# Four of the eight first-layer tiles as three one-pass products of 12-bit halves

## The chip, the core and the metric

The kernel runs on one core of a Trainium2 chip. Its engines are TensorE (PE, matmuls; PEld is its weight load), VectorE (DVE), ScalarE (ACT), GpSimd (POOL) and SyncE (SP, which only issues DMA transfers). Matmuls accumulate in PSUM; everything else lives in SBUF, 128 partitions wide. The metric is the device time of one execution in microseconds (us); the median of three runs is given. A line such as L687 is line 687 of the kernel. Where a helper issues every instruction of one kind, all of these carry the helper's line: L687 is `matmul`, L676 is the wrapper `Ordered` around VectorE and ScalarE, L707 is `special` (table functions of ScalarE).

## The reference

A gated linear recurrence over 768 steps for 4 x 8 heads of 48, then a two-layer feed-forward block on 3072 rows of 384:

```python
for t in range(S):
    new_re = ar * S_re - ai * S_im
    new_im = ar * S_im + ai * S_re
    S_re, S_im = (new_re + kv, new_im)          # kv = outer(k_t, v_t)
    y[:, :, t] = einsum('bhd,bhde->bhe', q[:, :, t], S_re)
x = y.transpose(0, 2, 1, 3).reshape(B * S, H * D)
h = x @ w_in            # 384 -> 2048
g = h * np.cos(h)
return (g @ w_out).astype(np.float32)   # 2048 -> 384
```

The gate per step is `a = a_re + i a_im`, its magnitude capped at 0.999. q, k, v and the gate come in float32, the weights of the block in float64.

## The kernel before

**Tiling.** The sequence is cut in 24 chunks of 128 steps, two chunks to a group, twelve groups (g = 0 to 11). Inside a chunk the recurrence is done as masked attention: the gates' running product is built from a logarithm (for the magnitude) and an arctangent (for the phase), each summed up over the steps by a matmul with a triangular matrix. Keys and queries are divided and multiplied by that product and stacked with the cosine and sine of the phase. Scores are `keys^T queries`, masked, times the values; between chunks a 96 x 48 state per head is carried.

**A group's work in order.** `log_steps` makes logarithm and angle (ScalarE and VectorE); `p_powers`, `even_steps` and `p_apply` the magnitude's products; `g_phase` sums the phases (tile `phs` on TensorE); `g_trig` makes cosine and sine, `g_stack` the stacked keys `ks` and queries `qs`. `f_transpose` turns them: a transpose in 32 x 32 blocks on VectorE (tile `tr`), a write to DRAM (`moved`), and reads back (`kT` in four transfers, `qT` in one). Then `f_scores` (tile `sc`), `f_out` (`yp`), `f_state` (`sp`), and through `f_x` and `f_xt` the rows `x` come back transposed as `xT`.

**First layer.** `mm1` makes one tile of h: for jp = 0 to 7, `mm1_sums` multiplies three 128-row slices of `w_in` with `xT` into an accumulator `hp` of 128 x 512 (2 x 256). There are three such accumulators, used in turn. A float32 matmul goes as two instructions, so a tile is 2 x 3 x 2 = 12 of them. `gate_sine` applies the sine (cosine by a shifted argument) and, with `Square`, keeps a check value; `gate_product` multiplies on VectorE into the tile `gate`.

**Second layer.** From group 2 (`PLAIN`) on, `g @ w_out` is one level of a seven-product scheme: 2 x 2 blocks of the gates (a11, a12, a21, a22) and of `w_out`. `mixed` makes the four mixed blocks s1 = a21 + a22, s2 = s1 - a11, s3 = a11 - a21, s4 = a12 - s2 for one pair of tiles; `seventh` is one half of one product.

**Order.** From group 2 on each turn of the last loop (L1568) hands a set of parts, each with a stretch of the turn (0.0 to 1.0), to `weave`, which issues them sorted by their place in it. In turn n TensorE does the attention of group n (`chunks`), the second layer of group n - 1 (`products`) and, from 0.56 on, the first layer of group n (`first`), while the other engines prepare group n + 1 (`logs`, `prods`, `phases`, `keys`). TensorE's instructions, ScalarE's table functions and GpSimd's instructions are chained in the order in which they are issued. For the rest of VectorE's and ScalarE's work and for the DMA queue the framework's planner sets the order: it takes, at the time it expects, the instruction that is ready and was issued first. A tile's home (a tag with `bufs` buffers) is given to the next tile of that tag only when all that read the last one are done.

**Guards.** The float64 weights are checked once more late in the kernel: `guarded` loads them again by GpSimd (tile `raw`, 768 KB each, two to a turn in groups 4 to 11), and VectorE and ScalarE test the exponents.

## Time and profile before

| | |
|---|---|
| runs (us) | 656.12, 653.86, 656.76; median 656.12 |
| profiled execution: span (us); the profile gives no other time of it | 651.2 |
| TensorE busy | 641.0 us, 98%, 4075 instructions |
| TensorE weight loads busy | 576.4 us, 89% |
| VectorE busy | 492.0 us, 76% |
| ScalarE busy | 392.8 us, 60% |
| GpSimd busy | 30.9 us, 5% |
| first layer (`hp`) on TensorE | 252.5 us busy, 1176 instructions |
| granted TensorE clock | 1.000 |

A row of the timeline reads: start, duration (us), engine, line, operation, output <- inputs, shape, count, and in brackets how long the engine had been idle before it and what released it. A row of the chain of waits reads: start, duration, engine, tile, count. A row of a table by stage reads: stretch and its length, then for PE, PEld, DVE, ACT and POOL the busy time with the number of instructions, then the granted clock, the mean busy share of the 16 DMA engines, and GB/s. A row of a group reads: line, engine, operation, output <- inputs, shapes, count | busy us, mean ns of one | idle time before it and its releaser. One of a single tile reads: count, least, median and greatest duration in ns, first and last start. Busy time counts overlapping instructions once, so it is less than count times mean.

### The profile page before, as it was taken

The page shows a single profiled execution, that of the slowest core. Times are in us where ns is not written, and L with a number is a line of the kernel's source. Part 1 is how long each engine was busy: PE and PEld are TensorE (multiplying, and loading weights), DVE is VectorE, ACT ScalarE, POOL GpSimd, SP SyncE. Part 2 cuts the span into 40 slices and gives each one's busy share as a digit, 9 for nine tenths or more (in the row PEclk, how much of TensorE's full clock was granted, in tenths as well). Part 3 has the DMA queues.
Part 4 walks back from the last instruction along what each step waited for, and adds up shares of the span by engine and source line. Part 5 has one row for each costly group of instructions (what it writes and reads, how often), then busy time and mean ns, then how long its engine had stood idle before and what let it go on. Part 6 is the DMA issues. An engine that isn't in the chain of part 4 may idle for free.

```text
span 651.2 us, 10758 instructions
## 1 busy us (share of the span) xinstructions
PE 641.0 (98%) x4075; PEld 576.4 (89%) x4075; DVE 492.0 (76%) x799; ACT 392.8 (60%) x726; POOL 30.9 (5%) x53
## 2 busy tenths in 40 slices
PE   8999999999999999999999999999999999999997
PEld 6888877777999999899899899899899999999996
DVE  6999989888687688786787787876877878862251
ACT  7898687284583593494494485485576476433330
POOL 4010200000000000010010010000000000000000
PEclk9999999999999999999999999999999999999999
DMA  9968755727627656747738737836836843363001
GB/s 249 244 179 203 225 164 123 170 62 182 146 49 182 158 146 148 194 110 167 209 82 191 204 85 167 205 96 151 226 105 146 219 123 98 112 134 120 25 1 31
DMA packets 232920, 94.90 MB, mean 146 GB/s; under 512 B 208701, under 2 KB 221246, under 8 KB 232858
## 3 DMA queue, kind: packets, MB, share of 16 engines
q1 hardware_dynamic: 225320, 68.51, 45.3%
q0 software_dynamic: 5824, 25.50, 11.7%
q8 instruction: 34, 0.56, 0.4%
q10 hardware_dynamic: 1714, 0.11, 0.2%
q14 instruction: 28, 0.23, 0.1%
HBM read 69.28 MB, written 24.81 MB: 144 GB/s over the span
## 4 chain that ended last, share of the span: by engine, by line
PE 92%; ACT 4%; DVE 3%; DMA 0%; issue 0%; SPq 0%; DVEq 0%
PE hp L687 38%; PE op L687 18%; PE sum L687 16%; PE sc L687 6%; PE yp L687 6%; PE sp L687 4%; PE phs L687 2%; PE lgs L687 1%; ACT tan L707 1%; PE yr L687 1%; PE tp L948 1%; ACT rs L707 1%; ACT lg L707 1%; ACT L703 1%; DVE mag L676 1%; DVE atm L676 1%
## 5 line engine op out<-in xcount | busy, mean ns | idle before, releaser
L687 PE MATMUL hp<-xT,w_in 128*128 128x256 f32 (+1 forms) x1176 | 252.5, 375 | 0.0
L687 PEld LDWEIGHTS hp<-xT,w_in 128*128 128x128 f32 x1176 | 219.6, 190 | 30.2 <-issue 0.2
L707 ACT ACTIVATE gate<-hp,half_pi_b 128x512 f32<-128x512 f32 x96 | 66.0, 687 | 118.5 <-PE hp L687 118.5
L687 PE MATMUL op<-w_out,gate 128*128 128x192 f32 (+1 forms) x448 | 100.7, 374 | 0.0
L676 DVE TENSOR_TENSOR gate<-hp,gate 128x512 f32<-128x512 f32 x96 | 65.7, 684 | 45.8 <-ACT junk L676 45.7
L687 PEld LDWEIGHTS op<-w_out,gate 128*128 128x128 f32 x448 | 75.9, 190 | 16.9 <-issue 2.0
L676 ACT ACTIVATE junk<-hp 128x512 bf16<-128x512 f32 x96 | 56.7, 591 | 0.0
L687 PE MATMUL sum<-t_s,s 128*128 128x192 f32 x320 | 56.3, 329 | 0.0
L687 PEld LDWEIGHTS sum<-t_s,s 128*128 128x128 f32 x320 | 52.1, 190 | 1.5 <-issue 1.5
L676 DVE TENSOR_TENSOR atm<-sc,causal 128x512 f32<-128x512 f32 x48 | 32.9, 689 | 23.4 <-PE sc L687 23.4
L687 PEld LDWEIGHTS sc<-qT,kT 96*128 96x128 f32 x384 | 47.4, 192 | 2.3 <-issue 0.6
L687 PE MATMUL sc<-qT,kT 96*128 96x128 f32 x384 | 49.0, 276 | 0.2 <-ACT qT L676 0.2
L676 ACT ACTIVATE ot<-sum 128x192 f32<-128x192 f32 x39 | 12.6, 322 | 53.7 <-PE sum L687 53.4
L676 DVE SCALAR_TENSOR_TENSOR ot<-op,ot 128x192 f32<-128x192 f32 x40 | 13.3, 354 | 38.0 <-PE op L687 36.4
L687 PE MATMUL yp<-atm,v 128*48 128x128 f32 x352 | 33.6, 277 | 0.9 <-ACT Q L707 0.6
L703 ACT ACT_TABLE_LOAD x24 | 30.8, 1283 | 1.2 <-PEq L1662 0.7
L676 ACT COPY yT<-yp 48x512 f32<-48x512 f32 x44 | 25.3, 574 | 7.4 <-PE yp L687 7.0
L687 PE MATMUL yp<-qT,state 96*48 96x128 f32 x304 | 29.7, 272 | 0.0
L687 PE MATMUL sum<-w_out,gate 128*128 128x192 f32 x160 | 29.7, 329 | 0.0
L687 PE MATMUL sp<-v,ks 128*96 128x48 f32 x320 | 29.7, 245 | 0.0
L687 PEld LDWEIGHTS sp<-v,ks 128*96 128x96 f32 x320 | 29.6, 165 | 0.0
L676 ACT CAST tan<-phs 128x384 int32<-128x384 f32 x24 | 11.4, 480 | 29.4 <-PE phs L687 29.4
(147 smaller groups left out, 987.4 us busy)
## 6 DMA issues: line engine op xcount, KB each, us to landing
moved<-tr SPq DMA_DIRECT2D x20, 768.0 KB
raw<-in_moe_w_in_dram POOLq DMA_DIRECT2D x16, 768.0 KB, 5.1
raw<-in_moe_w_out_dram POOLq DMA_DIRECT2D x16, 768.0 KB, 4.6
kT<-moved SPq DMA_DIRECT2D x40, 192.0 KB
qT<-moved SPq DMA_DIRECT2D x10, 768.0 KB
k<-in_k_dram SPq DMA_DIRECT2D x24, 192.0 KB
q<-in_q_dram SPq DMA_DIRECT2D x24, 192.0 KB
v<-in_v_dram SPq DMA_DIRECT2D x24, 192.0 KB
```

The lines of the kernel that those rows point to most:

```text
L676: ins = getattr(self.engine, op)(**kw)
L687: chain(nc.tensor.matmul(out, **kw), "tensor")
L703: chain(nc.scalar.preload_act_table_set(table))
L707: chain(nc.scalar.activation(func=func, **kw))
L948: chain(nc.tensor.transpose(ps[:, h], X[g][name[0] + "s"][:, x0 + h].rearrange("p a d -> p (a d)"), ident), "tensor")
```

## The change

From certain groups on, four of the eight tiles of the first layer (jp = 4 from group 2, 5 and 6 from group 3, 7 from group 4) are computed from halves. Weights and rows are cut, by a bit mask, into an upper half of 12 significant bits and the exact rest: w = wh + wl, x = xh + xl. Three products replace the float32 one, all in the one-pass type `float32r`: with S = 4096, `ps = wh xh + (S wl) xl` and `pb = (wh - S wl)(xh - S xl)`; then `ps - pb / (S + 1)` is `S / (S + 1)` times w x, and the factor `1 + 1/S` goes into the scale of the sine and of the gate product. A tile is then 2 x 3 x 3 = 18 one-pass instructions. `pb` takes one of the five general PSUM buffers (`hb`). ScalarE copies it with its factor, VectorE adds it (`whole_sum`), then sine and product go on.

The rows' halves are made once a group by `x_halves`: a mask and a subtraction, a three-operand mix (VectorE) and a copy (ScalarE). They live in the homes `lg`, `lo` and `rs` and the mask's result in `yT`'s. The weights' halves (`three_halves`) are made once, in turns 2, 3 and 4.

For room, other tiles share homes. Of the mixes only s1 has a tile of its own; s3 goes in place of a21, and `mixed_again` later puts s2 in place of a11 and s4 in place of a12. `qs` shares a home with the masked scores `atm`, the transposed queries' `tr` with `mag` and Q (`pair`), the guards' `raw` and the weights' mask with the keys' `tr`. The first layer's order goes from 0, 4, 1, 5, 2, 6, 3, 7 to 0, 1, 4, 2, 5, 3, 6, 7, two of the seven products change places, and the guards move from 0.1 - 0.9 of a turn to 0.68 - 0.98.

```diff
@@ -625,7 +626,8 @@
         _, a, b = src.shape
-        raw = stage["pool"].tile([C, a, b], I64, tag="raw", name="raw", bufs=stage["bufs"])
+        pool, tag = (ft, "tr") if stage["bufs"] == 1 else (stage["pool"], "raw")
+        raw = pool.tile([C, a, b], I64, tag=tag, name="raw", bufs=stage["bufs"])
         chain(nc.gpsimd.dma_start(out=raw, in_=src), "gpsimd")
...
@@ -737,8 +739,10 @@
                 x["sin"] = temp("tan", 2)
-            for name in "lg", "tan", "rs", "mag":
+            for name in "lg", "tan", "rs":
                 x[name] = temp(name, 2 if name == "tan" else 1)
+            both = gt.tile([C, 2, G * DM], F32, tag="pair", name="pair")
+            x["Q"], x["mag"] = both[:, 0], both[:, 1]
         m2, sq, rs, mag = (cut(x[name], i, n) for name in ("lg", "tan", "rs", "mag"))
...
@@ -909,8 +913,9 @@
         if i == 0:
-            for name in "ks", "qs":
-                x[name] = gt.tile([C, G * H, 2, D], F32, tag=name, name=name)
+            x["ks"] = gt.tile([C, G * H, 2, D], F32, tag="ks", name="ks")
+            pool, tag = (ft, "atm") if g else (stage["pool"], "qs")
+            x["qs"] = pool.tile([C, G * H, 2, D], F32, tag=tag, name="qs", bufs=1)
         for name, product in ("ks", "Q"), ("qs", "mag"):
...
@@ -924,7 +929,8 @@
                                  tag=name, name=name, bufs=1)
-        tr = ft.tile([C, NB, n * H, 32], F32, tag="tr", name="tr")
+        pool, tag = (ft, "tr") if name == "kT" else (gt, "pair")
+        tr = pool.tile([C, NB, n * H, 32], F32, tag=tag, name="tr", bufs=1)
         turn = vector.transpose(out=tr, in_=X[g][name[0] + "s"][:, ds(i * H, n * H)].rearrange(
...
@@ -956,9 +962,10 @@
     def f_scores(n, hh):
-        y = Y[n]
-        if hh == 0:
-            y["atm"] = ft.tile([C, H, C], F32, tag="atm", name="atm")
+        y, (g, i) = Y[n], divmod(n, G)
+        if i == 0 and hh == 0:
+            X[g]["atm"] = ft.tile([C, G, H, C], F32, tag="atm", name="atm", bufs=1)
+        y["atm"] = X[g]["atm"][:, i]
         ps = pa.tile([C, HH, C], F32, tag="a", name="sc")
...
@@ -1069,26 +1076,119 @@
         ps = x["hp"][jp]
+        if three(g, jp):
+            return mm1_three(g, jp, ps)
         lo, n = (0, G) if i is None else (i, 1)
             for dc in range(ND):
-                matmul(ps[:, ji, ds(lo * C, n * C)], lhsT=w_in[:, jp, dc, ts(ji, C)],
+                matmul(ps[:, ji, ds(lo * C, n * C)], lhsT=w_in[jp][:, dc, ts(ji, C)],
                        rhs=x["xT"][:, dc, ds(lo, n)].rearrange("p g t -> p (g t)"),
                        start=(dc == 0), stop=(dc == ND - 1))
+    def halves(g):
+        if g == PLAIN:
+            for name in "wl", "wx":
+                right[name] = stage["pool"].tile([C, len(THREE), ND, 256], F32R, name=name)
+        for n, jp in enumerate(THREE):
+            if FROM[jp] == g:
+                yield from three_halves(jp, right["wl"][:, n], right["wx"][:, n])
+    def three_halves(jp, wl, wx):
+        cut_ = ft.tile([C, ND, 256], F32, tag="tr", name="cut", bufs=1)
+        w = w_in[jp]
+        vector.tensor_scalar(out=cut_.bitcast(U32), in0=w.bitcast(U32), scalar1=UPPER,
+                             scalar2=None, op0=ALU.bitwise_and)
+        yield
+        vector.tensor_tensor(out=wl, in0=w, in1=cut_, op=ALU.subtract)
+        w_in[jp] = wts.tile([C, ND, 256], F32R, tag=f"w_in{jp}", name="wh", bufs=1)
+        scalar.copy(out=w_in[jp], in_=cut_)
+        yield
+        vector.scalar_tensor_tensor(out=wx, in0=wl.bitcast(F32), scalar=-SHIFT, in1=cut_,
+                                    op0=ALU.mult, op1=ALU.add)
+        scalar.mul(out=wl, in_=wl.bitcast(F32), mul=SHIFT)
+    def x_halves(g):
+        x = X[g]
+        def all_of():
+            return x["xT"].rearrange("p c g t -> p (c g t)")
+        def upper():
+            whole = all_of()
+            for name, tag in ("xx", "lg"), ("xl", "lo"), ("xh", "rs"):
+                x[name] = gt.tile([C, G * DM], F32R, tag=tag, name=name)
+            x["cut"] = ft.tile([C, G * DM], F32, tag="yT", name="cut", bufs=1)
+            vector.tensor_scalar(out=x["cut"].bitcast(U32), in0=whole.bitcast(U32), scalar1=UPPER,
+                                 scalar2=None, op0=ALU.bitwise_and)
+            scalar.copy(out=x["xh"], in_=x["cut"])
+        def lower():
+            vector.tensor_tensor(out=x["xl"], in0=all_of(), in1=x["cut"], op=ALU.subtract)
+        def apart():
+            vector.scalar_tensor_tensor(out=x["xx"], in0=x["xl"].bitcast(F32), scalar=-SHIFT,
+                                        in1=x["cut"], op0=ALU.mult, op1=ALU.add)
+        return [upper, lower, apart] if g >= PLAIN else []
+    def three(g, jp):
+        return g >= FROM.get(jp, NG)
+    def mm1_three(g, jp, ps):
+        x, k = X[g], THREE.index(jp)
+        x.setdefault("hb", {})[jp] = pb = pa.tile([C, 2, G * C], F32, tag="a", name="hb")
+        xh, xl, xx = (x[name].rearrange("p (c t) -> p c t", c=ND)
+                      for name in ("xh", "xl", "xx"))
+        wh, wl, wx = w_in[jp], right["wl"][:, k], right["wx"][:, k]
+        for ji in range(2):
+            for dc in range(ND):
+                matmul(pb[:, ji], lhsT=wx[:, dc, ts(ji, C)], rhs=xx[:, dc],
+                       start=(dc == 0), stop=(dc == ND - 1))
+        for ji in range(2):
+            for w, t, dc in [(w, t, dc) for w, t in ((wh, xh), (wl, xl)) for dc in range(ND)]:
+                matmul(ps[:, ji], lhsT=w[:, dc, ts(ji, C)], rhs=t[:, dc],
+                       start=(w is wh and dc == 0), stop=(w is wl and dc == ND - 1))
+    def whole_sum(g, jp, gate):
+        x = X[g]
+        ps = x["hp"][jp]
+        scalar.mul(out=gate, in_=x["hb"].pop(jp), mul=-1.0 / (SHIFT + 1.0))
+        vector.tensor_tensor(out=ps, in0=ps, in1=gate, op=ALU.add)
     def gate_sine(g, jp):
         ps = x["hp"][jp]
+        size = (1.0 + 1.0 / SHIFT if three(g, jp) else 1.0) / in_scale
         gate = x["gate"][jp] = msb.tile([C, 2, G * C], F32, tag="gate", name="gate", bufs=8)
         junk = msb.tile([C, 2, G * C], BF16, tag="junk", name="junk", bufs=1)
-        special(out=gate, in_=ps, func=AF.Sin, scale=1.0 / in_scale, bias=half_pi_b)
-        scalar.activation(out=junk, in_=ps, func=AF.Square, scale=1.0 / in_scale,
+        if three(g, jp):
+            whole_sum(g, jp, gate)
+        special(out=gate, in_=ps, func=AF.Sin, scale=size, bias=half_pi_b)
+        scalar.activation(out=junk, in_=ps, func=AF.Square, scale=size,
                           accum_out=wide[:, ds(g * (NJ // 2) + jp, 1)])
         gate = x["gate"][jp]
-        gated = vector.tensor_tensor(out=gate, in0=x["hp"].pop(jp), in1=gate, op=ALU.mult)
+        if three(g, jp):
+            gated = vector.scalar_tensor_tensor(
+                out=gate, in0=x["hp"].pop(jp), scalar=1.0 + 1.0 / SHIFT, in1=gate,
+                op0=ALU.mult, op1=ALU.mult)
+        else:
+            gated = vector.tensor_tensor(out=gate, in0=x["hp"].pop(jp), in1=gate, op=ALU.mult)
         x.setdefault("gated", gated)
...
@@ -1115,6 +1215,8 @@
+    FROM, UPPER, SHIFT = {4: 2, 5: 3, 6: 3, 7: 4}, 0xFFFFF000, 4096.0
+    THREE = sorted(FROM)
     PLAIN, HJ, E2 = 2, NJ // 2, DM // 2
...
@@ -1141,12 +1243,16 @@
         a11, a21, a12, a22 = lo[:, :, 0:C], lo[:, :, C:2 * C], hi[:, :, 0:C], hi[:, :, C:2 * C]
-        s = stage["pool"].tile([C, 3, 2, C], F32, tag="s", name="s", bufs=HJ // 2)
-        s1, s2, s4 = (s[:, i] for i in range(3))
-        for out_, a, b, op in ((s1, a21, a22, ALU.add), (s2, s1, a11, ALU.subtract),
-                               (a21, a11, a21, ALU.subtract), (s4, a12, s2, ALU.subtract)):
-            vector.tensor_tensor(out=out_, in0=a, in1=b, op=op)
-        X[g].setdefault("mix", {})[p] = {"s1": s1, "s2": s2, "s3": a21, "s4": s4}
+        s1 = stage["pool"].tile([C, 2, C], F32, tag="s", name="s", bufs=HJ // 2)
+        vector.tensor_tensor(out=s1, in0=a21, in1=a22, op=ALU.add)
+        vector.tensor_tensor(out=a21, in0=a11, in1=a21, op=ALU.subtract)
+        X[g].setdefault("mix", {})[p] = {"s1": s1, "s2": a11, "s3": a21, "s4": a12}
+    def mixed_again(g, p, name):
+        mix = X[g]["mix"][p]
+        a, b = ("s1", "s2") if name == "s2" else ("s4", "s2")
+        vector.tensor_tensor(out=mix[name], in0=mix[a], in1=mix[b], op=ALU.subtract)
     SEVEN = "a11", "a12", "a22", "s2", "s3", "s1", "s4"
...
@@ -1205,10 +1311,18 @@
         return [lambda p=p, part=part: seventh(g, p, part)
-                for p in (0, 1, 3, 2, 5, 4, 6)[lo:hi] for part in range(2)]
+                for p in (0, 1, 2, 3, 5, 4, 6)[lo:hi] for part in range(2)]
     def mixes(g, lo, hi):
         return [lambda p=p: mixed(g, p) for p in range(lo, hi)] if g >= PLAIN else []
+    def mixes_again(g, name):
+        return [lambda p=p: mixed_again(g, p, name) for p in range(HJ // 2)] if g >= PLAIN else []
+    def stepwise(part, count):
+        part = iter(part)
+        return [lambda: next(part, None) for _ in range(count)]
     def weave(*parts):
...
@@ -1268,7 +1382,7 @@
     def first(g):
-        order = range(NJ // 2) if g < PLAIN else (0, 4, 1, 5, 2, 6, 3, 7)
+        order = range(NJ // 2) if g < PLAIN else (0, 1, 4, 2, 5, 3, 6, 7)
         return [lambda jp=jp: mm1(g, jp) for jp in order]
...
@@ -1569,11 +1683,14 @@
               (prods(n + 1), 0.25, 0.27), (second(n - 1, 1), 0.36, 0.5),
+              (mixes_again(n - 1, "s2"), 0.24, 0.34), (mixes_again(n - 1, "s4"), 0.37, 0.48),
               (products(n - 1, 2 + (n < NG - 1), 7), 0.4, 0.56),
+              (stepwise(halves(n), 3 * list(FROM.values()).count(n)), 0.1, 0.5),
+              (x_halves(n), 0.598, 0.612),
               (phases(n + 1), *((0.472, 0.476) if n == PLAIN else (0.516, 0.524))),
               (last_quarter() if n == PLAIN else [], 0.9, 1.0), (first(n), 0.56, 1.0),
-              (mixes(n, 0, 2), 0.9, 1.0), (guarded(n - 1, per) if n > 3 else [], 0.1, 0.9))
+              (mixes(n, 0, 2), 0.9, 1.0), (guarded(n - 1, per) if n > 3 else [], 0.68, 0.98))
     checked = verdict(late, temp)
...
```

Left out of the diff: `w_in` as eight tiles in place of one, Q's move into the pair's home, the two products' places inside `seventh`, and the same two parts in the last `weave`.

16 lines of the change are left out of this document (9 added, 7 removed).

## The prediction

> **What bounds the kernel now.** I read the page's busy times first, then the chain of waits, then three engines' timelines over one group.
>
> ```profile
> span 651.2 us, 10758 instructions
> PE 641.0 (98%) x4075; PEld 576.4 (89%) x4075; DVE 492.0 (76%) x799; ACT 392.8 (60%) x726; POOL 30.9 (5%) x53
> ```
>
> TensorE is busy for 98% of the span, so whatever shortens its instruction stream can shorten the kernel, as long as its operands still arrive in time. The profile gives its execution a span of 651.2 us and no other time; the runs' median, 656.12 us, lies 4.9 us above it, and I add these 4.9 us to every sum. One turn of the steady state, from the chain that ended last:
>
> ```profile
> 352.44 1.05 PE phs L687 x6
> 353.49 2.60 PE sum L687 x16
> 356.09 20.72 PE hp L687 x96
> 376.81 0.89 PE sc L687 x8
> ...
> 403.64 1.05 PE phs L687 x6
> ```
>
> A group takes 403.64 - 352.44 = 51.2 us here, and the first layer (hp) 20.72 us of it: eight tiles, 2.59 us each, 96 instructions at 0.216 us. Between the phase sums (phs) and the next group's scores (sc) TensorE has 376.81 - 353.49 = 23.3 us of work. Meanwhile the other engines must turn those sums into the transposed keys and queries that sc reads. That second path is the one to watch. VectorE first, then the DMA queue of SyncE:
>
> ```profile
> 349.19 0.95 DVE L676 TENSOR_TENSOR mag<-q,lg 128x768 f32<-128x768 f32 x1
> 352.47 0.62 DVE L676 SCALAR_TENSOR_TENSOR ot<-op,ot 128x192 f32<-128x192 f32 x2 [2.33 <-PE op L687]
> 353.34 1.26 DVE L676 TENSOR_TENSOR tan<-phs,tan 128x384 f32<-128x384 f32 x2 [0.24 <-ACT tan L676]
> 354.70 0.56 DVE L676 TENSOR_SCALAR rs<-tan 128x768 uint32<-128x768 uint32 x1
> ...
> 357.25 0.95 DVE L676 TENSOR_TENSOR qs<-mag,rs 128x768 f32<-128x768 f32 x1
> 358.12 0.95 DVE L676 TENSOR_TENSOR qs<-mag,lo 128x768 f32<-128x768 f32 x1
> 358.99 0.17 DVE L676 TENSOR_SCALAR end<-end 96x16 f32<-96x16 f32 x1
> 359.07 2.25 DVE L676 STREAM_TRANSPOSE tr<-ks 128x1536 f32<-128x1536 f32 x1
> 361.23 0.14 DVE L676 SCALAR_TENSOR_TENSOR least<-end,least 96x16 f32<-96x16 f32 x1
> 361.28 0.69 DVE L676 TENSOR_TENSOR gate<-hp,gate 128x512 f32<-128x512 f32 x1
> 361.88 2.25 DVE L676 STREAM_TRANSPOSE tr<-qs 128x1536 f32<-128x1536 f32 x1
> 364.05 0.66 DVE L676 TENSOR_TENSOR gate<-hp,gate 128x512 f32<-128x512 f32 x1
> ```
>
> ```profile
> 361.34 3.15 SPq L933 DMA_DIRECT2D moved<-tr  x2
> 364.71 5.16 SPq L936 DMA_DIRECT2D kT<-moved  x4
> 369.98 1.25 SPq L938 DMA_DIRECT2D qT<-moved  x1
> ```
>
> ```profile
> 374.00:376.00 2.00, 2.00 (x11) 1.75 (x10) 1.66 (x5) 1.27 (x3) 0.00 (x0) 1.00 0.64 142
> 376.00:378.00 2.00, 2.00 (x15) 1.92 (x14) 0.51 (x2) 1.15 (x3) 0.00 (x0) 1.00 0.00 0
> ```
>
> The chain runs: phase sums end at 353.49; VectorE subtracts, ScalarE makes sine and cosine, VectorE multiplies keys and queries by them until 358.99, transposes the keys from 359.07 and the queries from 361.88 to 364.1; SyncE writes both to memory, reads the keys back in four transfers and the queries in one, issued at 369.98. DMA traffic ends close to 376.0, and TensorE reaches sc at 376.81. So the transposed queries are only some 0.8 us early. Within a group two paths of almost the same length lie side by side: 23.3 us of TensorE, 22.5 us of VectorE and DMA.
>
> **The matmuls.** The change alters 36 tiles: jp 4 in groups 2 to 11 (10), jp 5 and 6 in 3 to 11 (9 each), jp 7 in 4 to 11 (8). Each loses 12 instructions of two passes and gains 18 of one pass over 256 columns. (hp's 0.216 us for 256 columns against the 0.175 for 384 in the rows below is what two passes against one look like.) The profile has one-pass matmuls of 384 and 512 columns, none of 256:
>
> ```profile
> 352.45 0.34 PE L687 MATMUL phs<-lo,exact 128*128 128x384 f32 x1
> 352.63 0.34 PE L687 MATMUL phs<-hi,alls 128*128 128x384 f32 x1
> 352.80 0.34 PE L687 MATMUL phs<-hi,exact 128*128 128x384 f32 x1
> ```
>
> ```profile
> 6.72 3.11 PE L687 MATMUL busy<-idle 128*128 128x512 f32 x13
> ```
>
> ```profile
> L687 PE MATMUL busy<-idle x51: 387/393/796, 1.5 to 20.6; 128*128 128x512 f32 x51
> ```
>
> ```profile
> L687 PEld LDWEIGHTS hp<-xT,w_in 128*128 128x128 f32 x1176 | 219.6, 190 | 30.2 <-issue 0.2
> L687 PEld LDWEIGHTS lgs<-hi,exact 128*128 128x128 f32 x20 | 3.8, 190 | 0.0
> ```
>
> 384 columns start 0.175 us apart, 512 columns (3.11 - 0.39) / 12 = 0.227. The line through both gives 0.123 us for 256, so a changed tile takes 18 x 0.123 = 2.21 us where it took 2.59: 0.38 us less, and 36 x 0.38 = 13.7 us in all. Bounds: below, the eight sc instructions (0.89 / 8 = 0.111 us, 128 columns in two passes, a fresh 128-column weight load each) give 2.00 us a tile, 21 us in all; above, the 384-column spacing gives 3.15 us, a loss of 20 us. I take 0.123, since both its rows are of the type used.
>
> The weight loads of one-pass operands last as long as the others (190 ns in both rows), and sc starts an instruction every 111 ns with such a load ahead of each, so loads hide behind running matmuls. The Trainium skill (TensorE: Matmul & The Clock Gate, Part 3, "The mechanism") says that weight loads overlap running matmuls only where the row groups differ. All of these tiles use one row group, so that rule would expose every load: a changed tile of at least 18 x 0.190 = 3.42 us. The sc row speaks against it. It is a rival below.
>
> **The other engines in the layer.** A changed tile adds a copy on ScalarE, an addition on VectorE, and makes its product a three-operand one; each group adds x_halves, the mask, the subtraction and the third operand on VectorE and a copy on ScalarE:
>
> ```profile
> L676 DVE TENSOR_TENSOR gate<-hp,gate 128x512 f32<-128x512 f32 x96 | 65.7, 684 | 45.8 <-ACT junk L676 45.7
> L676 ACT ACTIVATE junk<-hp 128x512 bf16<-128x512 f32 x96 | 56.7, 591 | 0.0
> L728 ACT ACTIVATE hi<-lg 128x768 fp32r<-128x768 f32 x10 | 8.3, 830 | 0.0
> L676 DVE SCALAR_TENSOR_TENSOR lo<-lg,hi 128x768 fp32r<-128x768 f32 x10 | 9.5, 952 | 0.0
> ```
>
> ```profile
> 400.00:450.00 50.00, 49.85 (x331) 46.22 (x330) 39.20 (x62) 31.70 (x59) 1.78 (x3) 1.00 0.63 157
> ```
>
> VectorE: 4 x 0.68 + 0.56 + 0.95 + 0.95 = 5.2 us a group on top of 39.2 in 50, so 44.4: under the period still. ScalarE: 4 x 0.59 + 0.83 = 3.2 on top of 31.7. The product's new form costs nothing (at 768 elements the form with a scalar takes 952 ns in the last row, the plain one 0.95 us at 349.19). Neither engine becomes the bound by its sum. The wait inside a tile grows: ScalarE's sine waits for the addition, which waits for the last matmul, some 0.7 us more before the accumulator is free; there are three accumulators and two tiles (4.4 us) between reuse, so that is covered; bounds 0 and 0.7 us a group. Behind the addition stand, on VectorE, gate products and mixes of this layer, which TensorE reads first in the second-layer products after sc. The in-place mixes are the same four operations; two move behind the products that read their homes, into the idle stretch ahead of 352.47 (2.33 us), price 0, or 8 x 0.34 = 2.7 us a group if that cover is gone (each has half the elements of a gate product). The weight halves (four times 0.56 + 0.95 + 0.95 us, once) fall in groups 2 to 4, where VectorE has its 20% of idle time: 0, bound 10 us if all were exposed.
>
> **What is put into the second path.** This is the step that decides. x_halves writes into the homes rs, lo and lg, and rs and lo hold cosine and sine until qs<-mag,lo has started at 358.12 and finished. So the subtraction and the third operand can't run before 358.99, whatever their place in the weave. There VectorE already has keys' transpose, a gate product and queries' transpose to do, and the new pair goes in among them: spacing of 128x768 operations 0.87 us, so 2 x 0.87 = 1.74 us (0.47 more if the mask isn't done earlier, in the 0.24 us gap and its like). Two instructions wait for what is pushed back:
>
> First, the third tile of the layer (jp 4) needs all three halves at 356.09 + 2 x 2.59 = 361.27. With the pair right behind 358.99 it is ready at 360.8: no stall. With the keys' transpose first (the weave puts it just ahead), at 361.23 + 1.74 + 0.1 = 363.1, and 0.6 later with the gate product between: a stall of 1.8 to 2.4 us.
>
> Second, in both orders queries' transpose ends 1.74 us later, and its write to memory stands on SyncE ahead of the four reads of the keys, which stand ahead of the read of the queries. So the last landing moves from about 376.0 to 377.7. Yet TensorE, with 4 x 0.38 = 1.5 us less to do, would be at sc by 375.3, or, after a stall at the third tile, at 377.1 to 377.7. Either way sc starts near 377.9 instead of 376.81: the group gets longer by about 1.1 us (the 1.74 less the 0.8 that was to spare, plus some 0.15 from landing to start), and the faster matmuls fill a wait. Bounds: +0.3 (the landing's slack fully used and the kT reads going ahead) and +2.4 (mask and gate product on the path too).
>
> **The sum.** Groups 2 to 10 each prepare a next group: 9 x 1.1 = +9.9 us. Group 11 prepares none and keeps its four tiles' gain, -1.5. Sum +8.4: a span of 659.6, a time of 664.5 us.
>
> **Rivals.**
>
> *The path doesn't bind, faster.* If the queries' delay is absorbed (the read at 369.98 follows the four key reads, whose 5.16 us don't depend on the second write if SyncE issues them first), and the halves are there at 361.27, the whole 13.7 us counts: 642.4. If the path keeps its old length, only its slack can be won: 9 x 0.8 + 1.5 = 8.7, so 647.4. For it: the slack of the second write, issued by 364.5 and read only at 369.98. Against it: both conditions are needed at once, and the third tile's deadline asks for the order that pushes keys back too. Chance 0.30, around 646.
>
> *The guards' traffic joins the path, slower still.* Their raw tile now shares the home tr with the keys' transpose, so a guard's 768 KB can start once that is written, in the middle of the reads of keys and queries:
>
> ```profile
> 381.50:383.50 2.00, 2.00 (x25) 1.77 (x25) 1.90 (x5) 1.97 (x4) 0.00 (x0) 1.00 0.93 272
> 383.50:385.50 2.00, 2.00 (x25) 1.81 (x22) 2.00 (x5) 2.00 (x4) 0.00 (x0) 1.00 0.33 129
> ```
>
> One such transfer, alone, fills the DMA engines for 2 x (0.93 + 0.33) = 2.5 us. Groups 4 to 10 (7) could lose up to that: 17.5, on top of the forecast 682. Chance 0.12.
>
> *The two balance.* The third tile's stall 1.8 against 1.5 saved, with the queries' reads overlapped: +0.3 x 9 - 1.5, within a few us of 656. Chance 0.16.
>
> *The products aren't faster.* Exposed weight loads (18 x 0.190 = 3.42 us a tile against 2.59): 36 x 0.83 = +30, 686. Chance 0.02. That one pass were no faster than two is excluded by the 384-column spacing.
>
> **The numbers.** The forecast has 0.40, at 664.5, its own range 659 to 672. A measurement of this kernel tells apart about 0.5%, 3.3 us. Faster takes the first rival and a little of the balance, 0.31; same 0.15; slower 0.54 (forecast, guards, loads). For 8 in 10 the range reaches into the fast case and into the guards' one: 643 to 682.
>
> **What would show it.** In the profile after: hp's two-pass instructions down by 36 x 12 = 432 from 1176; 648 one-pass instructions 0.12 us apart (0.11 right too, 0.19 for exposed loads). TensorE's busy share under 96%, with idle time at the third tile (released by VectorE's xx) or ahead of sc (released by the queries' landing), 2 to 3 us a group; VectorE's pair between 359 and 364 in this group's terms. I am wrong if TensorE stays at 98% and the period falls below 50 us, or if queries' transpose isn't later relative to the layer's start.

## The result and the profile after

| | before | after |
|---|---|---|
| median of four runs (us) | 655.91 | 746.25 (745.18 to 746.80) |
| profiled execution: span (us) | 651.2 | 744.5 |
| TensorE busy | 641.0 us, 98% | 662.3 us, 89% |
| mean granted TensorE clock | 1.000 | 0.952 |

The ratio is 1.138, with a 95% interval of 1.135 to 1.140: slower, as forecast, but by 90 us where I forecast 8, and far above the top of the range (682). Busy times, and from the chain that ended last its shares by engine:

```profile
span 744.5 us, 11395 instructions
...
PE 662.3 (89%) x4291; PEld 597.3 (80%) x4291; DVE 544.5 (73%) x877; ACT 422.1 (57%) x780; POOL 33.3 (4%) x53
...
PE 56%; DVE 17%; ACT 9%; DMA 8%; issue 7%; SPq 1%; ACTq 0%; DVEq 0%; POOL 0%; POOLq 0%
```

The chain that ended last is TensorE's own work for only 56%, where it was 92% before. Where TensorE stood idle, by groups of instructions (the last figures are the idle time ahead of the group and its releaser):

```profile
L689 PE MATMUL hp<-xT,w_in 128*128 128x256 f32 (+1 forms) x744 | 165.4, 377 | 1.5 <-DVE ot L678 1.0
...
L689 PE MATMUL hb<-xx,wx 128*128 128x256 f32 x216 | 39.8, 325 | 35.0 <-DVE xx L678 33.0
...
L689 PE MATMUL sc<-qT,kT 96*128 96x128 f32 x384 | 50.0, 279 | 5.3 <-DMA qT<-moved 5.1
...
L689 PE MATMUL sum<-t_s,s 128*128 128x192 f32 x160 | 33.3, 369 | 15.8 <-DVE ot L678 15.8
```

hp's two-pass instructions are down by 432 to 744, as the change says. Two places hold most of the idle time: the first product in halves, waiting for VectorE's xx, and a product of the second layer, waiting for VectorE's readout ot. One group on TensorE:

```profile
382.55 2.76 PE L689 MATMUL sum<-t_s,gate 128*128 128x192 f32 x16
387.92 2.87 PE L689 MATMUL sum<-t_s,s 128*128 128x192 f32 x16 [2.61 <-DVE ot L678]
...
396.87 5.34 PE L689 MATMUL hp<-xT,w_in 128*128 128x256 f32 x24
407.12 1.60 PE L689 MATMUL hb<-xx,wx 128*128 128x256 f32 x6 [4.91 <-DVE xx L678]
```

and on VectorE, with the rows behind which the two waits end:

```profile
386.65 0.95 DVE L678 TENSOR_TENSOR pair<-q,lg 128x768 f32<-128x768 f32 x1
387.52 0.35 DVE L678 SCALAR_TENSOR_TENSOR ot<-sum,ot 128x192 f32<-128x192 f32 x1
...
399.07 0.95 DVE L678 TENSOR_TENSOR qs<-pair,lo 128x768 f32<-128x768 f32 x1
399.94 2.27 DVE L678 STREAM_TRANSPOSE tr<-ks 128x1536 f32<-128x1536 f32 x1
402.13 0.52 DVE L678 TENSOR_SCALAR cut<-xT 128x768 uint32<-128x768 uint32 x1
402.56 0.69 DVE L678 TENSOR_TENSOR gate<-hp,gate 128x512 f32<-128x512 f32 x1
403.16 0.95 DVE L678 TENSOR_TENSOR xl<-xT,cut 128x768 fp32r<-128x768 f32 x1
404.03 2.20 DVE L678 STREAM_TRANSPOSE tr<-qs 128x1536 f32<-128x1536 f32 x1
406.15 0.92 DVE L678 SCALAR_TENSOR_TENSOR xx<-xl,cut 128x768 fp32r<-128x768 f32 x1
```

The mask, the subtraction and the mix stand around both transposes, so that xx is ready 10.2 us after the layer's start at 396.87, where TensorE could have used it after 5.2. Further on in the same group a guard (the first row is GpSimd's issue, the second SyncE's):

```profile
405.98 0.74 POOL L631 DMA_DIRECT2D raw<-in_moe_w_in_dram  x1 [24.84 <-DMA moved<-tr]
```

```profile
406.67 7.79 SPq L942 DMA_DIRECT2D kT<-moved  x4
```

```profile
424.27 0.56 DVE L678 TENSOR_SCALAR raw<-raw 128x768 uint32<-128x768 uint32 x1 [3.87 <-DMA raw<-in_moe_w_in_dram]
424.75 0.69 DVE L678 TENSOR_TENSOR hp<-hp,gate 128x512 f32<-128x512 f32 x1
```

The guard's 768 KB start when the keys' tr has been written out, and the four reads of the keys beside them take 7.79 us (5.16 before). The next guard lands late, and VectorE stands 3.87 us in front of it with the layer's additions behind.

### The profile page after: what moved, and what is told of

The parts are those of the page before. It is cut to its first block, busy times and chain, and to the rows that moved or that the text cites. A ratio compares the mean times of both kernels' runs of the same rounds, so it can differ in the third digit from the quotient of the medians.

```text
span 744.5 us, 11395 instructions
## 1 busy us (share of the span) xinstructions
PE 662.3 (89%) x4291; PEld 597.3 (80%) x4291; DVE 544.5 (73%) x877; ACT 422.1 (57%) x780; POOL 33.3 (4%) x53
## 4 chain that ended last, share of the span: by engine, by line
PE 56%; DVE 17%; ACT 9%; DMA 8%; issue 7%; SPq 1%; ACTq 0%; DVEq 0%; POOL 0%; POOLq 0%
PE hp L689 18%; PE op L689 13%; PE sum L689 7%; PE sc L689 4%; PE yp L689 4%; PE hb L689 3%; DMA raw<-in_moe_w_out_dram 3%; PE sp L689 2%; DVE pair L678 2%; DVE ks L678 2%; DVE tr L678 2%; DMA qT<-moved 2%; DMA raw<-in_moe_w_in_dram 2%; PE phs L689 2%; DVE tan L678 2%
## 5 line engine op out<-in xcount | busy, mean ns | idle before, releaser
L689 PE MATMUL hp<-xT,w_in 128*128 128x256 f32 (+1 forms) x744 | 165.4, 377 | 1.5 <-DVE ot L678 1.0
L689 PEld LDWEIGHTS hp<-xT,w_in 128*128 128x128 f32 x744 | 138.3, 193 | 20.9 <-DVE ot L678 1.4
L689 PE MATMUL hb<-xx,wx 128*128 128x256 f32 x216 | 39.8, 325 | 35.0 <-DVE xx L678 33.0
L689 PEld LDWEIGHTS hb<-xx,wx 128*128 128x128 f32 x216 | 32.6, 209 | 39.5 <-DVE xx L678 29.0
L689 PE MATMUL sum<-w_out,gate 128*128 128x192 f32 x304 | 55.5, 331 | 0.0
L689 PEld LDWEIGHTS sum<-w_out,gate 128*128 128x128 f32 x304 | 50.4, 193 | 0.0
L678 DVE SCALAR_TENSOR_TENSOR gate<-hp,gate 128x512 f32<-128x512 f32 x36 | 24.8, 688 | 29.9 <-ACT junk L678 29.9
L678 DVE TENSOR_TENSOR hp<-hp,gate 128x512 f32<-128x512 f32 x36 | 25.1, 696 | 26.7 <-PE hp L689 26.6
L689 PE MATMUL hp<-xh,wh 128*128 128x256 f32 x216 | 41.8, 307 | 0.0
L689 PE MATMUL hp<-xl,wl 128*128 128x256 f32 x216 | 41.4, 304 | 0.0
```

The lines of the kernel that those rows point to most:

```text
L678: ins = getattr(self.engine, op)(**kw)
L689: chain(nc.tensor.matmul(out, **kw), "tensor")
```

## Experiments

The theories: (P) the prediction's, the path from phase sums to scores with x_halves in it; (G) the guards; (S) the second layer's order; (H) the shared homes and in-place mixes. The expectations call S also A; T is the part of P at the third tile (the rows' halves come late for it); L is a VectorE that simply has too much to do, so that a wait taken away comes back elsewhere. An execution's wait totals below are from the view of waits: idle us, times, longest.

**no_halves**: all eight tiles float32, the rest of the change stays.

```diff
...
-    FROM, UPPER, SHIFT = {4: 2, 5: 3, 6: 3, 7: 4}, 0xFFFFF000, 4096.0
+    FROM, UPPER, SHIFT = {}, 0xFFFFF000, 4096.0
...
```

> The changed kernel with no tile in halves: all eight tiles float32 as before, no rows' or weights' halves; the shared homes, the mixes in place, the guards' places and both new orders stay. A: what is left over the kernel before is the wait at the accumulator, 10 x 1 to 2.3 us: 666-680. T: no wait at the third tile. L: with VectorE's load back to that of before nothing waits: 656-661. If the shared homes or the guards' transfers cost something by themselves, it is over 680.

Measured 716.41 us (1.091, 1.083 to 1.098). A miss: two thirds of the loss stand without any half. VectorE's waits for the guards:

```profile
DVE raw L678 <- DMA raw<-in_moe_w_out_dram: 43.0, 8, 11.9
...
DVE raw L678 <- DMA raw<-in_moe_w_in_dram: 36.2, 8, 6.1
```

**sums_apart**: the changed kernel with the second layer's products and readouts in the old order (the mixes s2, which are then needed earlier, at 0.13 to 0.25).

```diff
...
-                for p in (0, 1, 2, 3, 5, 4, 6)[lo:hi] for part in range(2)]
+                for p in (0, 1, 3, 2, 5, 4, 6)[lo:hi] for part in range(2)]
...
```

> The changed kernel with the second-layer products in the order before (a11, a12, s2, a22, s1, s3, s4), so that no two products follow each other in the accumulator called sum; s2 is mixed earlier for that. Theory A (the accumulator): in the changed kernel s2 and s1 follow each other in it, and the first matmul of s1 waits for VectorE to read s2 out; 10 such waits and the half clock behind them cost 22.7 us of TensorE's time. Without them 746 falls to 722-732. Theory T (the rows' halves are late for the third tile of the first layer) expects its own 36.5 us unchanged. Rival L (VectorE is simply overloaded, and a wait taken away comes back at the next place): 741 or more.

Measured 707.69 us (1.077, 1.063 to 1.092): 38.6 us come back, give or take some 10 (two runs, 704.21 and 711.16). That is more than the 14 to 24 us expected, and L (741 or more) is out. The earlier place of the mixes s2 is part of the edit, and its share isn't separated.

**before_sums**: the kernel before with only that order of products and readouts changed.

```diff
...
-                for p in (0, 1, 3, 2, 5, 4, 6)[lo:hi] for part in range(2)]
+                for p in (0, 1, 2, 3, 5, 4, 6)[lo:hi] for part in range(2)]
```

> The kernel before with one part of the change alone: the order of the second-layer products (a11, a12, a22, s2, s1, s3, s4), with the readouts that go with it. A: one wait of TensorE per group for VectorE's readout of s2, 10 x 0.7 to 2.6 us: 663-682. L (the wait is there only when VectorE is late): 656-660.

Measured 675.95 us (1.029, 1.022 to 1.036). The kernel before took 657.01 us in the same set of runs, so the order costs 19 us with nothing else changed. Its row of waits:

```profile
PE sum L687 <- DVE ot L676: 16.5, 10, 4.1
```

s2 and s1 both sum in the one accumulator `sum`. In the old order a product of another accumulator stood between them (before, on TensorE):

```profile
341.77 2.87 PE L687 MATMUL sum<-t_s,s 128*128 128x192 f32 x16
344.47 2.76 PE L687 MATMUL op<-t_a,gate 128*128 128x192 f32 x16
347.07 2.76 PE L687 MATMUL sum<-t_s,s 128*128 128x192 f32 x16
```

In the new one s1 follows s2 at once and must wait until s2 has been read out, now by VectorE, where that readout stands behind the magnitude's products (386.65, then 387.52, in the rows of the result). The edit does two things at once: it puts s1 next to s2, and it hands s2's readout from ScalarE to VectorE. No run has one without the other.

**no_guards**: the changed kernel without guards (that check is left out).

```diff
-    guards = [src for _, src in into + back if src.dtype != F32]
+    guards = []
...
```

> The changed kernel without the guards (the second load of the weights and the test of their exponents are left out). Theory G: their transfers now start right behind the keys' transpose, and they cost twice: they share the DMA engines with the reads of keys and queries, and VectorE and ScalarE, which work in order, stand still until they land. In no_halves, where the halves are out of it, the waits of the scores, of yp and of lgs came to some 35 us beyond those of the kernel before. Without guards 746 falls by 25-40 us, to 706-721, and the waits of VectorE for raw (31 us) are gone. Rival: the third tile's wait takes up most of it (it waits for VectorE anyway): under 12 us, 734 or more.

Measured 711.29 us (1.085, 1.082 to 1.088): 35 us less.

**guards_back**: the changed kernel with the guards earlier in the turn, still in the shared home.

```diff
-              (mixes(n, 0, 2), 0.9, 1.0), (guarded(n - 1, per) if n > 3 else [], 0.68, 0.98))
+              (mixes(n, 0, 2), 0.9, 1.0), (guarded(n - 1, per) if n > 3 else [], 0.1, 0.5))
```

> The changed kernel with the guards at 0.1-0.5 of a turn, ahead of the keys' transpose that shares their home, so that their transfers run where those of the kernel before did. G: as good as without guards within 8 us, 706-728. Rival (sharing one home is what costs, wherever the guards stand, since the keys' transpose then waits for them): 740 or more.

Measured 719.81 us (1.098, 1.094 to 1.101): 26.4 of the 35 us come back by their place alone.

**guards_untested**: in their new place, transfers without the test.

```diff
-        vector.tensor_scalar(out=e, in0=e, scalar1=1, scalar2=21,
-                             op0=ALU.logical_shift_left, op1=ALU.logical_shift_right)
-        scalar.activation(out=e.bitcast(F32), in_=e, func=AF.Relu, scale=-1.0, bias=least_e_b,
-                          accum_out=odd[:, ds(next(odds), 1)])
```

> The changed kernel with the guards' transfers in their new place but without the test of the exponents behind them (the shift on VectorE and the sum on ScalarE are left out, so that check is not made); the raw tiles still land in the home shared with the keys' transpose. The changed kernel takes 746.25 us, without any guards 711.29. If what costs is that VectorE and ScalarE stand in order behind a landing that comes late, this run takes 708 to 716 us. If it is the transfer itself, among the reads of keys and queries, or the home that it holds against the next transpose, it takes 735 to 746 us. In between: both.

Measured 733.98 us (1.119, 1.116 to 1.123), in between: the transfers with the home that they hold cost about 22.7 us (733.98 - 711.29), VectorE and ScalarE standing in order behind them 12.3. SyncE's rows give most of the 22.7 us to the transfers. One group's reads of the keys, in no_guards and in guards_untested:

```profile
394.04 4.75 SPq L942 DMA_DIRECT2D kT<-moved  x4
```

```profile
403.92 7.06 SPq L938 DMA_DIRECT2D kT<-moved  x4
```

In the seven groups with a guard beside them these reads take 53.9 us in all, without guards 35.5, 18.5 us less. VectorE stands idle ahead of no keys' transpose, so a delay by the home doesn't show as a wait; that it pushes other work back isn't excluded. What TensorE then waits for is the transposed queries, a wait that no_guards has not among its longest:

```profile
PE sc L685 <- DMA qT<-moved: 15.3, 5, 5.2
```

**homes_alone**: no halves, old product order, no guards (that check is left out); the shared homes, the in-place mixes and the first layer's new order stay.

```diff
...
-    FROM, UPPER, SHIFT = {4: 2, 5: 3, 6: 3, 7: 4}, 0xFFFFF000, 4096.0
+    FROM, UPPER, SHIFT = {}, 0xFFFFF000, 4096.0
...
-                for p in (0, 1, 2, 3, 5, 4, 6)[lo:hi] for part in range(2)]
+                for p in (0, 1, 3, 2, 5, 4, 6)[lo:hi] for part in range(2)]
...
-    guards = [src for _, src in into + back if src.dtype != F32]
+    guards = []
...
```

> The changed kernel with all tiles float32, the second-layer products in the order before, and without guards (their test is left out): only the shared homes, the mixes in place and the first layer's new order are left of the change. If these cost nothing: 648-658 (the kernel before, less a little for the guards). If the homes bring waits of their own: 662 or more, with the tile that waits named in the trace.

Measured 655.58 us (0.999, 0.997 to 1.001). H is out beside float32 tiles: there these parts cost nothing. Beside the halves no run has them apart.

**halves_first**: the changed kernel with the pair earlier and the keys' transpose put behind xx.

```diff
+        if name == "kT" and "made" in X[g - 1]:
+            behind(turn, X[g - 1]["made"])
...
-              (x_halves(n), 0.598, 0.612),
+              (x_halves(n), *((0.55, 0.57) if n == PLAIN else (0.575, 0.59))),
```

> The changed kernel with the rows' halves made ahead of the keys' transpose on VectorE (issued earlier, and the transpose put behind the third operand xx). T: the wait of the third tile, 36.5 us in nine groups, falls under 5 us. Theory P (the path of the prediction: phase sums to transposed queries is full, whatever stands on it): both transposes and the transfers behind them are 2 to 3 us later instead, so most of the gain comes back as a wait of the scores for the queries; 728-736 us in all. If the path has room (T alone), the whole 36 us is won: 705-715. L: 741 or more.

Measured 733.18 us (1.116, 1.108 to 1.125). The wait for xx nearly goes (0.5 us), and the next instruction in line waits in its place:

```profile
PE sc L689 <- DMA qT<-moved: 28.6, 6, 5.6
```

What is gained at the third tile is lost at sc: both hang on one stretch of VectorE's work, as P says. The size of the new wait isn't P's alone, though. The guards' transfers are still beside the reads of the keys (6.4 to 7.3 us in the seven groups that have them, 5.1 in the group ahead of these), and without a guard the wait by the starts of the matmuls is 1.4 us, with one 4.2 to 5.7.

**path_alone**: S undone, the guards earlier, P left; nearly the case that the prediction had summed (edits of sums_apart and guards_back). The guards stand at 0.1 to 0.5 of a turn, though, and not at the 0.1 to 0.9 of the kernel before, as the expectation says.

> The changed kernel with two of its edits undone and nothing else: the second layer's products and readouts in the old order, and the guards' words over the old stretch of the group. The halves, the masks, the pair of vectors and the places of phases and transposes stay. This is the case that the prediction had summed. If its sum holds (18 + 9 x 1.1 - 1.5 - 18 us around it): 664.5 us. If the groups' first four tiles still wait for the pair as they did with both edits undone singly (26 to 35 us at the third tile, 16.8 at the scores), while the two undone edits give back what they gave singly (38.5 and 26.4 us): about 681 us, 670 to 700, with 25 to 45 us of waits at the third tile and the scores. Should the two undone edits overlap in what they give back, more than 690.

Measured 684.49 us (1.046, 1.044 to 1.049). The two edits together give 61.8 of the 90 us back (singly 38.6 and 26.4). no_halves says the same from the other side: with both edits and no halves 60.5 of the 90 us are left (716.41 - 655.91). One group, VectorE and TensorE; this layer starts at 477.87:

```profile
481.00 2.25 DVE L678 STREAM_TRANSPOSE tr<-ks 128x1536 f32<-128x1536 f32 x1
...
483.21 0.56 DVE L678 TENSOR_SCALAR cut<-xT 128x768 uint32<-128x768 uint32 x1
...
483.88 0.96 DVE L678 TENSOR_TENSOR xl<-xT,cut 128x768 fp32r<-128x768 f32 x1
...
484.75 0.68 DVE L678 TENSOR_TENSOR gate<-hp,gate 128x512 f32<-128x512 f32 x1
...
485.36 0.95 DVE L678 SCALAR_TENSOR_TENSOR xx<-xl,cut 128x768 fp32r<-128x768 f32 x1
486.22 2.26 DVE L678 STREAM_TRANSPOSE tr<-qs 128x1536 f32<-128x1536 f32 x1
486.36 0.77 PEld L689 LDWEIGHTS hb<-xx,wx 128*128 128x128 f32 x6 [3.55 <-DVE xx L678]
486.36 0.96 PE L689 MATMUL hb<-xx,wx 128*128 128x256 f32 x6 [3.15 <-DVE xx L678]
```

This is the order that the prediction had with the keys' transpose first and the gate product between, with the mask in it too.

**mended**: path_alone, with phases, keys' transposes and x_halves earlier in the turn.

```diff
-              (x_halves(n), 0.598, 0.612),
-              (phases(n + 1), *((0.472, 0.476) if n == PLAIN else (0.516, 0.524))),
-              (keys(n + 1), *((0.5, 0.62) if n == PLAIN else (0.53, 0.64))),
+              (x_halves(n), 0.556, 0.568),
+              (phases(n + 1), *((0.432, 0.436) if n == PLAIN else (0.452, 0.456))),
+              (keys(n + 1), *((0.46, 0.6) if n == PLAIN else (0.47, 0.6))),
```

> The changed kernel with the products in the order before, the guards at 0.1-0.5, and the phase sums with what hangs on them (keys, queries, rows' halves) issued 5 seventh-parts ahead of the first layer, where it was 2. P (phase sums to queries is the full path, and only its place binds): with 3.9 us more room neither the third tile nor the scores wait, and the 15 us of faster matmuls show: 640-652. If the halves cost VectorE more than it has: 656-680, with waits spread over its readers. If only the two waits taken away count and the place doesn't: 680-700.

Measured 668.51 us (1.019, 1.017 to 1.022), in the range for a VectorE that has less room than the halves ask; P's 640 to 652 is missed. The place counts all the same: 16 us less than path_alone, and no wait of the scores. The third tile still waits, 10.1 us in all in this row:

```profile
PE hb L689 <- DVE xx L678: 10.1, 7, 1.8
```

**mended_late**: mended, the tiles in their natural order, so four float32 tiles stand ahead of the first in halves.

```diff
-        order = range(NJ // 2) if g < PLAIN else (0, 1, 4, 2, 5, 3, 6, 7)
+        order = range(NJ // 2) if g < PLAIN else (0, 1, 2, 3, 4, 5, 6, 7)
```

> The mended kernel (668.5 us) with the first layer's tiles in the order 0 to 7, so that four float32 tiles of 2.59 us stand ahead of the first tile in halves where two stood. If the 14.8 us of waits between hp and hb are only the pair coming late, they go, and the time is about 654 us (650 to 658), with the 15.6 us of shorter products first seen in the time. If VectorE as a whole is what is late there (it is busy nearly without a gap through that part of the group), the wait goes to the gates and the second layer's readouts (yp, lgs, hb behind hb), and the time stays at 662 to 670 us.

Measured 653.82 us (0.999, 0.997 to 1.001). The wait is gone.

**mended_none**: mended with FROM empty, no halves made.

> The mended kernel with no tile in halves: all eight tiles float32, no weights prepared, no vectors cut; the order of everything else as in the mended kernel. If the places of the guards, phases and transposes cost nothing, as the shared homes and the mixes did: 655 to 657 us, like before. If the earlier phases cost or gain, it shows here: 645 to 653 or 659 to 668 us. Beside it the mended kernel with tiles 0 to 7 gives what the halves alone are worth.

Measured 654.67 us (0.9995, 0.998 to 1.001), like before. So the mended places cost nothing beside float32 tiles, the shared home of the guards included. The halves in mended_late are worth 0.9 us, which the runs (651.91 to 656.69 with, 653.68 to 657.24 without) can't tell from nothing.

**late_no_guards**: mended_late without guards (that check is left out).

> The mended kernel with tiles 0 to 7 and without guards (no transfer, no test of the exponents: that check is left out). With them it took 653.82 us though its products are 14.4 us shorter than those of the same kernel without halves (654.67 us). If the waits that take this gain are still the guards' (xT landing late, lgs and yp behind raw): 645 to 649 us. If they come from the rest (VectorE's extra work of 5 us a group, the homes that the halves hold until the last tile): 651 to 654 us.

Measured 644.36 us (0.982, 0.980 to 0.985). Without guards the halves are worth 655.58 - 644.36 = 11.2 us (homes_alone is the other; the mended places, in which it differs, cost nothing). The guards cost nothing beside float32 tiles (654.67 with, 655.58 without) and 9.5 us beside the halves.

**late_split** and **late_spread**: mended_late with three float32 tiles ahead and the fourth last (0, 1, 2, 4, 5, 6, 7, 3), or with the guards over 0.1 to 0.9; **split_spread** has both.

> The mended kernel with the first layer's tiles in the order 0, 1, 2, 4, 5, 6, 7, 3: three float32 tiles ahead of the first in halves, and a float32 tile last, so that the homes of the halves come free a tile (2.6 us) earlier than with 0 to 7. If the waits of the next group's sums (lgs, released by lo, 4.7 and 2.7 us in all) come from those homes, they go, and the time is 648 to 652 us. If VectorE is simply late there: 653 to 656 us; and if three tiles are too few for the pair, waits between hp and hb come back, 655 to 660 us.

> The mended kernel with tiles 0 to 7 and the guards over 0.1 to 0.9 of a turn, as in the kernel before, in place of 0.1 to 0.5. If only a late second guard harms (behind the transposes), this one is like the changed kernel's place: 658 to 672 us. If the two guards harm by standing close together: 648 to 652 us.

> The mended kernel with both of the last single edits: the tiles in the order 0, 1, 2, 4, 5, 6, 7, 3 (alone 649.75 us) and the guards over 0.1 to 0.9 of a turn (alone 649.69 us). Without guards the kernel with tiles 0 to 7 took 644.36 us. If the two edits take away different waits (the order yields the tiles' and lgs, the guards' place the landings of xT), the gains of about 4 us each add: 645 to 647 us. If both take away the same lateness of VectorE behind the guards: 649 to 651 us, with yp waiting for atm as in each of them (6 to 11 us).

Measured 649.75 us (0.990, 0.987 to 0.993), 649.69 (0.992, 0.989 to 0.995) and 649.48 (0.992, 0.990 to 0.994). All three beat both kernels, the one before by 5 to 6 us, and the two edits don't add. In late_split TensorE is busy for 97% of its span again, and the waits that are left stand elsewhere (here for the masked scores):

```profile
PE yp L689 <- DVE atm L678: 7.1, 13, 1.0
```

The waits of lgs for lo, which late_split was to test, fall from 4.7 and 2.7 us (weight loads and matmuls) to 2.9 and 1.4: homes coming free earlier are the smaller part of its gain.

## Why the prediction was wrong in size

**The step that failed: edits costed at nothing.** The prediction wrote "the in-place mixes are the same four operations", priced them at 0, and summed only "what is put into the second path". The mixes do cost nothing beside float32 tiles (homes_alone). What stood beside them in the change, the order of the products, had no term at all, though two sums in one accumulator now followed each other: 19 us by before_sums, 38.6 in the changed kernel. With the guards' new place this is 61.8 of the 82 us that the forecast lacks (746.25 - 664.5). The other 20 are in path_alone, below.

**The guards.** They were a rival, at 0.12, with the right place (the home tr, in the middle of the reads) and at most 2.5 us for each of seven groups. It happened, and costs 35 us in place of 17.5. The price was that of one transfer, and the reads of the keys did slow by about that: 18.5 us in the seven groups. It left out the test: 12 us by guards_untested, from VectorE and ScalarE standing in order. It also priced one of the two guards of a turn. And it had a chance of 0.12 and no term in the sum.

**"The matmuls"** held. In late_split, TensorE's timeline from the start of an hb to that of the next tile (372.08 to 374.22) is a whole tile:

```profile
372.08 0.88 PE L689 MATMUL hb<-xx,wx 128*128 128x256 f32 x6
372.80 0.52 PE L689 MATMUL hp<-xh,wh 128*128 128x256 f32 x3
373.15 0.51 PE L689 MATMUL hp<-xl,wl 128*128 128x256 f32 x3
373.50 0.52 PE L689 MATMUL hp<-xh,wh 128*128 128x256 f32 x3
373.86 0.52 PE L689 MATMUL hp<-xl,wl 128*128 128x256 f32 x3
374.22 1.03 PE L689 MATMUL hp<-xT,w_in 128*128 128x256 f32 x4
```

2.14 us where 2.21 was forecast, 0.119 us an instruction: 0.45 x 36 = 16.2 us saved, for 13.7. (Two more counts stand in the expectations: 15.6 from the same starts in the changed kernel, 14.4 from the sum over all matmuls.) The rival of exposed weight loads (3.42 us a tile) is out. The rule that I had put from the Trainium skill (TensorE: Matmul & The Clock Gate, Part 3, "The mechanism") doesn't hold for these tiles. Another sentence of that section also lets a load go ahead into a background weight buffer. The trace agrees with that sentence: loads of 190 ns hide behind matmuls 119 ns apart.

**"What is put into the second path"** named the right place. In path_alone the third tile waits 3.15 us in the group shown, for a forecast of 1.8 to 2.4: the mask was not made earlier, and 0.67 us of it is in the row (483.21 to 483.88). By the starts of all matmuls these waits come to 25.4 us over nine groups, 2.8 each. Against 16.2 us of shorter products that is +9.2 us, close to the +8.4 of the sum by luck. For the sc wait, on which the sum had put the end, hardly came (2.5 us): the late third tile covers it, until halves_first takes that away. In the changed kernel the queries' transpose went in as well, ahead of xx (404.03), and the wait is 4.91. The sum's "9 x 1.1" was right in size by a different wait.

**What path_alone still lacks** is 684.49 - 664.5 = 20 us. A stall was priced at its idle time only; the clock behind it was not. The mean granted clock of path_alone is 0.986: 681.0 x 0.014 = 9.5 us, an estimate. TensorE's busy time says much the same: its 4291 instructions take 636.5 us here and 628.4 in late_split, whose clock is 0.998. For the changed kernel the estimate gives 744.5 x 0.048 = 36 us, the busy times 662.3 - 628.4 = 34. These 34 us don't come on top of the edits' costs: they are the part of the 90 us that stands behind the stalls, whichever edit makes them. Of the remaining 10 us of path_alone a part may be the guards, since guards_back, which has them in the same place, is still 8.5 us above no_guards (719.81 - 711.29). The rest stands in small waits for VectorE and DMA (lgs, yp, xT). No run separates these.

**"The other engines"**: VectorE's 44.4 us in 50 fits by the sum, as the prediction had it, but not in order. The last runs take waits away one after the other, and each time TensorE waits at another place, for VectorE in the main: in mended for xx (10.1 us), in mended_late for the landing of xT (3.5) and for lo (2.7), in late_split for atm (7.1).

## What to carry to other kernels

In this kernel VectorE had a tenth of its time free by the sum (44.4 us in 50) and was late all the same, since its order is fixed: whatever is put ahead of a path, or may wait for a transfer, delays all that is behind it. Look at every reordering of sums in one accumulator and ask who reads it out, and behind what. Price the parts of a change that are "only moved" with the same care as the new operations; here they held 62 of 90 us.

## What the runs showed of the hardware

After a stall the granted clock can fall to half. In the changed kernel it does so sixteen times before the last instructions, for 3.41 us or twice that, and any two of these falls begin a whole number of 3.413 us apart (the first four at 202.41, 222.89, 263.85 and 280.91: 6, 12 and 5 times 3.413). So the clock seems to be set anew for each stretch of one fixed grid. Three places by stretches of that grid (stretch and length, busy time of PE, PEld, DVE, ACT and POOL, granted clock, DMA share, GB/s):

```profile
198.99:202.41 3.42, 0.92 (x6) 0.92 (x6) 2.45 (x4) 0.00 (x0) 0.00 (x0) 1.00 0.44 111
202.41:205.82 3.41, 3.41 (x12) 3.41 (x12) 0.00 (x0) 0.00 (x0) 0.00 (x0) 0.50 0.88 156
...
383.31:386.73 3.42, 2.00 (x13) 1.70 (x11) 3.42 (x5) 0.47 (x2) 0.00 (x0) 1.00 0.00 1
386.73:390.14 3.41, 2.22 (x13) 2.22 (x14) 1.14 (x3) 0.00 (x0) 0.00 (x0) 1.00 0.74 128
390.14:393.55 3.41, 3.41 (x23) 3.41 (x22) 0.12 (x1) 0.33 (x1) 0.00 (x0) 1.00 1.08 244
...
403.79:407.21 3.42, 0.09 (x1) 0.09 (x1) 3.42 (x4) 0.95 (x3) 0.74 (x1) 1.00 0.39 158
407.21:410.62 3.41, 3.41 (x16) 3.41 (x17) 0.46 (x1) 0.60 (x1) 0.00 (x0) 0.50 0.97 244
```

The last stall, of 4.9 us, leaves TensorE 0.09 us of work in one stretch, and the next runs at half the clock. The tile behind it takes 3.76 us (407.12 to 410.88) in place of 2.14, so the stall costs 1.6 us more than it shows. The other two are stalls of the same length ahead of the same product:

```profile
201.49 4.55 PE L689 MATMUL sum<-t_s,s 128*128 128x192 f32 x16 [2.61 <-DVE ot L678]
```

```profile
387.92 2.87 PE L689 MATMUL sum<-t_s,s 128*128 128x192 f32 x16 [2.61 <-DVE ot L678]
```

The first (198.88 to 201.49) lies almost wholly in one stretch, which keeps 0.92 us of work; the clock halves, and the 16 instructions take 4.55 us. The second (385.31 to 387.92) falls on two stretches, which keep 2.00 and 2.22 us; the clock stays, and they take 2.87. The Trainium skill (TensorE: Matmul & The Clock Gate, Part 1, "What's actually happening") explains it by a window of about 3.4 us that runs freely: a whole idle window halves the clock until a busy one has passed. The trace agrees in the 3.41 us and in that the place decides. It differs in that the window need not be wholly idle: one with 0.92 us of work halved the clock as well.
